# Attention in an MoE kernel: the last V product contracts over 128 rows, one group of maxima moves behind the first V product, high parts are made a head ahead, the division moves into odd heads

## The chip, the cores and the metric

The kernel runs on one core of a Trainium2 chip. The metric is the device time of one execution in microseconds (us); less is better. Five engines work side by side, each through its own program in order: TensorE (PE, matrix products; its weight loads are shown apart as PEld), VectorE (DVE), ScalarE (ACT), GpSimd (POOL) and SyncE (SP), which here issues the DMAs.

## The reference, cut to what matters

The program is a causal attention over blocks of 64 positions, an MoE with a cosine as its activation, and a second MoE with a normalised gate. The change touches the attention alone.

```python
def _attn_ref(q, k, v):                 # 4 batches, 8 heads, 576 positions, 64 wide
    scores = scale * np.matmul(q, k.transpose(0, 1, 3, 2))
    mask = block_i >= block_j           # blocks of 64
    scores = np.where(mask, scores, -1000000000.0)
    scores = scores - np.max(scores, axis=-1, keepdims=True)
    attn = np.exp(scores)
    attn = attn / (np.sum(attn, axis=-1, keepdims=True) + 1e-09)
    return np.matmul(attn, v)

x = attention laid out as (2304, 512)
h = x @ w_in; x = (h * np.cos(h)) @ w_out          # first MoE
out = sum over 8 experts of P[:, e] * (relu(x @ w1[e]) @ w2[e])   # second MoE
```

## The kernel before, in words

**Heads.** `attention()` walks the 32 heads (4 batches x 8) in one loop, `for i in range(NH)`, written out by hand: the order of the calls in its body is the order of the instructions on each engine, and semaphores do the rest. A head has 576 positions, that is four chunks of 128 keys and a fifth of 64. The scores stand transposed (keys in partitions, queries in columns), so a row sum comes out of the V product through a column of ones in `V`.

**Two passes for precision.** q and k are split into a high part in the short format that one PE pass takes (fp32r) and the rest. `high_parts(i)` makes the high parts of head `i` from the loaded tile `st[i]`: `HI` (both of them, ACT), `QA` (ACT), `KA` and `KB`'s lower half (two casts on POOL). `low_parts(i)` writes `QB = st - HI` on DVE. `move_q_hi` and `move_k_lo` bring halves to other partitions by DMA (`qb<-qa`, `kb<-qb`). The product of QB and KB (128 rows) and that of QA and KA (101 rows) add up in PSUM.

**The maxima** for head i+1 are found while head i is worked on. `peak(i + 1, 0)` and `peak(i + 1, 1)` are two groups of three short products into the one PSUM tile `px`; `find` reduces each with two and three instructions `nm<-px` on DVE. The second group writes over the first, so it waits for the first `find`. `turn` transposes the result on PE (`pt`), and `maxima` writes it, negated by a product with `diag`, into rows 96 to 100 of QA, where the QA-KA product subtracts it.

**Weights and V product.** `weights(i, 0..3)` compute the score tiles `sp`, `sq`, `sr` (512 columns each) and `sc` (the last 64 keys), and ACT takes their exponentials into `EP`, `EQ`, `ER` and `EC`. `pv(i, 0..4)` multiplies these by V. They are plain f32 products, so each counts twice in the trace (two passes). `EC` is a 64x64 tile, and its product uses 64 contraction rows. Even heads write 65 output rows, odd heads 128.

**Division.** `evac` copies a finished head from PSUM, `sums` sends its row sums to DRAM, `fetch`, `invert` and `give` take the reciprocals, `spread` brings them back over 64 partitions as `RB`, and `scale(e, h)` multiplies a head by them (DVE, two inputs in SBUF), for both heads of a pair. `x_hi` and `x_lo` split the outcome for the first MoE.

**Side work.** `conv_gen` converts the weights of the first MoE in small steps, of which `some(1)` issues the next: ACT `magnitude` together with the load of the next piece (`cw`, 512 KB, from SP), then ACT `rounding` and DVE `clamp`, then DVE `shift` and `bits`, then POOL `add`. One piece takes four steps, and four steps are issued per pair of heads. SP issues in each head, in program order: the `cw` load, V, two loads of q and k, `sums`, `qb<-qa`, `tt<-inv` (the spread), `kb<-qb`, as far as the head has them.

## Time and profile before

| | |
|---|---|
| Time, median of 3 runs | 2161.98 us (2161.3 to 2164.63) |
| The profiled execution's own time | 2162.53 us |
| Its span in the trace | 2160.7 us |
| PE busy | 2136.2 us (99%) |
| DVE, ACT, POOL busy | 1486.6, 961.9, 888.5 us (69%, 45%, 41%) |
| Chain that ended last | PE 86%, issue 5%, DVE 4%, POOL 3% |

The span runs from the first to the last instruction; the time of an execution holds 1.83 us more. Attention is the first tenth of the span: the first product of the MoE starts at 217.55 us. The granted PE clock is full in all slices of the page.

### The profile page before, as it was taken

The numbers are of one execution on the slowest core, as the hardware profiler recorded it, in microseconds if no ns is written. First come the engines' busy times: TensorE is split into PE (matmuls) and PEld (weight loads), VectorE is DVE, ScalarE is ACT, GpSimd is POOL, SyncE is SP. The second block draws the span as 40 slices with busy tenths as digits, with TensorE's granted clock in tenths as the row PEclk, the third lists the DMA queues.
The fourth block names the chain that finished last, engine by engine and source line by source line (L and its number), as shares of the span: only waits on it lengthen the run. The fifth ranks groups of instructions, "written<-read, shape, count | busy, mean of one in ns | idle before, by whom it ended". The sixth has DMA issues, their size and how long they took to land.

```text
span 2160.7 us, 29639 instructions
## 1 busy us (share of the span) xinstructions
PE 2136.2 (99%) x10869; PEld 1878.3 (87%) x10869; DVE 1486.6 (69%) x2445; ACT 961.9 (45%) x1795; POOL 888.5 (41%) x809
## 2 busy tenths in 40 slices
PE   8999999999999999999999999999999999999999
PEld 6666899998988889898888989888898888888898
DVE  7888677567667866666767666666766666666666
ACT  6777555434444433433444343444334344433432
POOL 3444444333324334344553434343563434344341
PEclk9999999999999999999999999999999999999999
DMA  6676220001002112121212212122122212212120
GB/s 157 181 182 170 65 69 20 7 1 40 1 22 70 66 60 78 59 79 59 73 65 88 78 59 79 59 72 66 60 77 88 78 59 71 67 61 77 59 78 30
DMA packets 74161, 152.84 MB, mean 71 GB/s; under 512 B 32896, under 2 KB 32896, under 8 KB 74016
## 3 DMA queue, kind: packets, MB, share of 16 engines
q1 hardware_dynamic: 74016, 150.95, 22.9%
q8 instruction: 86, 1.41, 0.3%
q14 instruction: 59, 0.48, 0.1%
HBM read 136.91 MB, written 4.87 MB: 66 GB/s over the span
## 4 chain that ended last, share of the span: by engine, by line
PE 86%; issue 5%; DVE 4%; POOL 3%; ACT 1%; DMA 1%; SPq 0%; POOLq 0%; ACTq 0%; DVEq 0%
PE acc L492 12%; PE acc L494 12%; PE acc L493 12%; PE hx L494 6%; PE hx L492 6%; PE hx L493 6%; PE acc L723 6%; PE hy L494 3%; PE hy L492 3%; PE hy L493 3%; POOL jl L68 2%; PE h L494 2%; PE h L492 2%; PE h L493 2%; PE hz L492 2%
## 5 line engine op out<-in xcount | busy, mean ns | idle before, releaser
L602 POOL TENSOR_TENSOR wv<-stg,wv 128x512 fp32r<-128x512 f32 x190 | 333.6, 1776 | 856.9 <-ACT wv L601 856.9
L492 PE MATMUL acc<-wv,hh 128*128 128x512 f32 x1152 | 456.5, 396 | 0.0
L494 PE MATMUL acc<-wv,hl 128*128 128x512 f32 x1152 | 455.5, 395 | 0.0
L493 PE MATMUL acc<-wv,hh 128*128 128x512 f32 x1152 | 454.5, 395 | 0.0
L897 DVE SCALAR_TENSOR_TENSOR oa<-acc,P,oa 128x512 f32<-128x512 f32 x540 | 379.0, 740 | 4.9 <-PE acc L494 4.3
L868 ACT ACTIVATE hh<-c 128x384 fp32r<-128x384 f32 x288 | 151.3, 525 | 409.5 <-DVE c L953 168.5
L869 DVE SCALAR_TENSOR_TENSOR hl<-c,hh 128x384 fp32r<-128x384 f32 x288 | 164.8, 572 | 176.1 <-ACT hh L868 176.1
L494 PEld LDWEIGHTS acc<-wv,hl 128*128 128x128 f32 x1152 | 216.0, 187 | 53.7
L493 PEld LDWEIGHTS acc<-wv,hh 128*128 128x128 f32 x1152 | 215.9, 187 | 43.9
L492 PEld LDWEIGHTS acc<-wv,hh 128*128 128x128 f32 x1152 | 216.1, 188 | 42.9
L68 POOL TENSOR_TENSOR jl<-raw,jh 128x512 fp32r<-128x512 f32 x95 | 132.2, 1393 | 190.0 <-ACT jh L65 178.2
L946 DVE TENSOR_TENSOR c<-hz,c 128x384 f32<-128x384 f32 x96 | 53.4, 557 | 193.9 <-PE hz L494 193.9
L593 DVE TENSOR_TENSOR wal<-s,wah 128x1024 fp32r<-128x1024 f32 x96 | 171.4, 1786 | 0.0
L936 ACT ACTIVATE c<-hx 128x384 f32<-128x384 f32 x95 | 46.9, 493 | 275.7 <-PE hx L494 275.7
L494 PE MATMUL hy<-xh,wal 128*128 128x384 f32 x384 | 128.8, 336 | 1.0 <-DVE wal L593 1.0
L492 PE MATMUL hy<-xh,wah 128*128 128x384 f32 x384 | 128.9, 336 | 0.6 <-DVE c L953 0.4
L492 PE MATMUL hx<-th,wah 128*128 128x384 f32 x384 | 128.6, 335 | 0.5 <-ACT c L936 0.5
L494 PE MATMUL hx<-th,wal 128*128 128x384 f32 x384 | 128.5, 335 | 0.0
L493 PE MATMUL hy<-xl,wah 128*128 128x384 f32 x384 | 128.3, 334 | 0.0
L493 PE MATMUL hx<-tl,wah 128*128 128x384 f32 x384 | 128.3, 334 | 0.0
L492 PE MATMUL h<-xh,jh 128*128 128x384 f32 x376 | 126.4, 336 | 0.5 <-PE h L494 0.5
L494 PE MATMUL h<-xh,jl 128*128 128x384 f32 x376 | 126.3, 336 | 0.4 <-POOL jl L68 0.4
(223 smaller groups left out, 4741.5 us busy)
## 6 DMA issues: line engine op xcount, KB each, us to landing
stg<-in_w_b_dram SPq DMA_DIRECT2D x192, 512.0 KB
cw<-in_w_a_dram SPq DMA_DIRECT2D x32, 512.0 KB
st<-in_qk_dram SPq DMA_DIRECT2D x64, 144.0 KB
v<-in_v_dram SPq DMA_DIRECT2D x31, 160.0 KB
tt<-inv SPq DMA_DIRECT2D x32, 144.0 KB
out_dram<-oa SPq DMA_DIRECT2D x18, 256.0 KB
kb<-qb SPq DMA_DIRECT2D x31, 144.0 KB
qb<-qa SPq DMA_DIRECT2D x31, 144.0 KB
```

The source lines that it names most:

```text
L68: eng_lo.tensor_tensor(out=lo, in0=src, in1=hi.bitcast(F32), op=ALU.subtract)
L492: nc.tensor.matmul(ps, lh, rh, start=first, stop=False, skip_group_check=go_on)
L493: nc.tensor.matmul(ps, lh, rl, start=False, stop=False, skip_group_check=go_on)
L494: nc.tensor.matmul(ps, ll, rh, start=False, stop=last, skip_group_check=go_on)
L593: eng.tensor_tensor(out=self.al, in0=self.s, in1=self.ah.bitcast(F32), op=ALU.subtract)
L602: eng.tensor_tensor(out=t[:, DM:2 * DM], in0=src, in1=t[:, 0:DM].bitcast(F32), op=ALU.subtract)
L723: nc.tensor.matmul(acc[half, b][:, at:at + w_], w[:, s], h[:, t0:t0 + w_], start=f == 0 and i == 0 and at == 0, stop=f == F1 - 1 and i == ...
L868: nc.scalar.activation(hh, src, AF.Relu)
L869: nc.vector.scalar_tensor_tensor(out=hl, in0=src, scalar=0.0, in1=hh.bitcast(F32), op0=ALU.max, op1=ALU.subtract)
L897: nc.vector.scalar_tensor_tensor(out=o, in0=acc, scalar=p, in1=o, op0=ALU.mult, op1=ALU.add)
L936: nc.scalar.activation(c[0], x, AF.Copy)
L946: nc.vector.tensor_tensor(out=c[0], in0=z, in1=c[0], op=ALU.add)
```

## The change

1. `EC` becomes one fixed tile of 128 rows, whose lower 64 rows are zeroed once by POOL; the last V product contracts over all 128 rows.
2. The second group of maxima (`peak(i + 1, 1)`) is issued behind `pv(i, 0)`, not ahead of it, and `pt` behind the product with the first part of `ER`, one product later than before.
3. `HI` is made by a function of its own, `high_both(i + 3)`, at the end of ACT's work in head i: the high part for a head is ready one head ahead. `low_parts(i + 2)`, which needs it, stands ahead of the second `find`.
4. Both `scale` calls stand in odd heads, one ahead of `low_parts`, one behind `maxima`.
5. The weight conversion has five steps a piece, the clamp being one of its own, and five are issued per pair of heads; they move so that the clamp falls in even heads, `add` and the `cw` load in odd heads. In the first MoE `some(4)` becomes `some(5)`.

```diff
@@ -136,8 +136,9 @@
                 if 0 < k < NHALF - 1:
                     self.load(k + 1)
                 yield
+                self.clamp(k)
+                yield
                 self.rounding(k)
-                self.clamp(k)
                 yield
                 self.shift(k)
                 self.bits(k)
@@ -166,6 +167,8 @@
             HI = p1.tile([128, S], F32R, name="hi")
             NM = [p1.tile([128, 101], F32, name=f"nm{j}") for j in range(2)]
             diag = p1.tile([128, 640], BF16, name="diag")
+            EC = p1.tile([128, D], F32, name="ec")
+            nc.gpsimd.memset(EC[64:128, :], 0.0)
 
             V = [p1.tile([128, 5, D + 1], F32, name="v0"), p1.tile([128, 5, 2 * D], F32, name="v1")]
             VC = [slice(0, D), slice(D, 2 * D)]
@@ -180,7 +183,7 @@
             conv = Conv(post.tile([128, 4 * DM], I32, tag="th", name="cw", bufs=1), tla[:, 0:DM].bitcast(I32))
             conv_gen = conv.run()
             SC = top.tile([72, 2, 8], F32, name="sc8")
-            st, EP, EQ, ER, EC, SUMS, INV, ps_t, ps_o = ({} for _ in range(9))
+            st, EP, EQ, ER, SUMS, INV, ps_t, ps_o = ({} for _ in range(8))
 
             def some(n):
                 for _ in range(n):
@@ -242,8 +245,10 @@
                 nc.gpsimd.memset(V[1][:, :, 0:D], 0.0)
                 nc.gpsimd.memset(V[1][:, :, 0:1], 1.0)
 
+            def high_both(i):
+                nc.scalar.activation(HI, st[i], AF.Copy)
+
             def high_parts(i):
-                nc.scalar.activation(HI, st[i], AF.Copy)
                 nc.scalar.activation(QA[i % 2][0:64, 64:640], st[i][64:128, :], AF.Copy)
                 nc.gpsimd.tensor_copy(out=KA[i % 2][0:64, :], in_=st[i][0:64, :])
                 nc.gpsimd.tensor_copy(out=KB[i % 2][64:128, :], in_=st[i][0:64, :])
@@ -332,8 +337,7 @@
                 else:
                     ps = pst.tile([128, 512], F32, tag="c", name="sc")
                     scores(ps[:, 0:256], i, 4, 320, 256)
-                    EC[i] = p1.tile([64, 64], F32, tag="ec", name="ec")
-                    nc.scalar.activation(EC[i], ps[0:64, 192:256], AF.Exp, scale=0.125)
+                    nc.scalar.activation(EC[0:64, :], ps[0:64, 192:256], AF.Exp, scale=0.125)
 
             def pv(i, c):
                 m = D + 1 if i % 2 == 0 else 2 * D
@@ -354,7 +358,7 @@
                     nc.tensor.matmul(o[:, 832:1024], vt[:, 3], ER.pop(i)[:, 320:512], start=False, stop=True,
                                      skip_group_check=True)
                 else:
-                    nc.tensor.matmul(o[:, 960:1024], vt[0:64, 4], EC.pop(i), start=False, stop=True,
+                    nc.tensor.matmul(o[:, 960:1024], vt[:, 4], EC, start=False, stop=True,
                                      skip_group_check=True)
 
             def evac(i):
@@ -416,6 +420,7 @@
             tiles()
             find(*px)
             find(*peak(0, 1))
+            high_both(1)
             high_parts(1)
             ones_of_v()
             turn(0)
@@ -433,8 +438,6 @@
                     load(i + 3)
                 if i:
                     sums(i - 1)
-                if even and i:
-                    some(1)
                 if nxt:
                     move_q_hi(i + 1)
                 if even and i >= 4:
@@ -443,37 +446,48 @@
                     find(*peak(i + 1, 0))
                 for part in range(4):
                     weights(i, part)
+                    if i == 0 and part == 0:
+                        high_both(2)
                 if odd and i >= 3:
                     invert(i - 3)
                     give(i - 3)
                 if odd and i >= 5:
-                    scale(i - 5, 1)
+                    scale(i - 5, 0)
+                if even and i:
+                    some(1)
+                if nxt2:
+                    low_parts(i + 2)
+                    move_k_lo(i + 2)
+                pv(i, 0)
                 if nxt:
                     find(*peak(i + 1, 1))
                 if nxt2:
                     high_parts(i + 2)
                 if even and i >= 2:
                     fetch(i - 2)
-                if nxt2:
-                    low_parts(i + 2)
-                    move_k_lo(i + 2)
+                if odd and i > 1:
+                    some(1)
                 if even and i >= 6:
                     x_hi(i - 6)
                     x_lo(i - 6)
+                if odd or i:
+                    some(1)
+                if i + 3 < NH:
+                    high_both(i + 3)
                 if i == NH - 1:
                     split(*spare, raw[0][:, 0:DM], nc.scalar, nc.gpsimd)
-                some(1)
-                pv(i, 0)
                 pv(i, 1)
+                pv(i, 2)
                 if nxt:
                     turn(i + 1)
                     maxima(i + 1)
-                for c in range(2, 5):
-                    pv(i, c)
-                if even and i >= 4:
-                    scale(i - 4, 0)
-                if odd:
+                pv(i, 3)
+                pv(i, 4)
+                if odd and i >= 5:
+                    scale(i - 5, 1)
+                if even and i:
                     some(1)
+            some(3)
             evac(NH - 1)
             sums(NH - 1)
             e = NH - 2
@@ -781,7 +795,7 @@
                         gb = times(pb, rb)
                         g_hi(n, 1, gb)
                         g_lo(n, 1, gb)
-                        some(4)
+                        some(5)
                     else:
                         wsplit(n - 1, 1)
                         open_group(0)
```

What it moves on PE, shown for head 21 (an odd head): from the end of its scores (`sc`) to the scores of the next head. `px` is the maxima tile, `o` the output of the V product. Before:

```order
L312 MATMUL sc<-qa_99,ka_101 64x256
L278 MATMUL px<-ka_100,qa_98 128x256
L278 MATMUL px<-ka_100,qa_98 128x320
L278 MATMUL px<-ka_100,qa_98 128x256
L345 MATMUL o<-ep,v_111 128x512
L346 MATMUL o<-eq,v_111 128x64
L348 MATMUL o<-eq,v_111 128x448
L299 MATMUL pt<-ident,nm_107 101x128
L351 MATMUL o<-er,v_111 128x320
L354 MATMUL o<-er,v_111 128x192
L357 MATMUL o<-ec,v_111 128x64
L278 MATMUL px<-ka_101,qa_99 128x256
```

After, in the same place:

```order
L317 MATMUL sc<-qa_99,ka_101 64x256
L349 MATMUL o<-ep,v_113 128x512
L350 MATMUL o<-eq,v_113 128x64
L283 MATMUL px<-ka_100,qa_98 128x256
L283 MATMUL px<-ka_100,qa_98 128x320
L283 MATMUL px<-ka_100,qa_98 128x256
L352 MATMUL o<-eq,v_113 128x448
L355 MATMUL o<-er,v_113 128x320
L304 MATMUL pt<-ident,nm_107 101x128
L358 MATMUL o<-er,v_113 128x192
L361 MATMUL o<-ec,v_113 128x64
L283 MATMUL px<-ka_101,qa_99 128x256
```

The three `px` products stand two V products later, and only two V products are left behind `pt`, where there were three.

On DVE, one pair of heads, from the first `find` of an odd head (two `nm<-px`) on; `tt` is the target of a scale, `qb<-st,hi` the low part, `qa<-pt,diag` the maxima. Before:

```order
L294 TENSOR_REDUCE nm_107<-px 128x1 x2
L375 RECIPROCAL sc_119<-sc_119 72x16
L392 TENSOR_TENSOR tt<-raw,tt 64x576
L294 TENSOR_REDUCE nm_107<-px 128x1 x3
L253 TENSOR_TENSOR qb_103<-st,hi 128x576
L113 TENSOR_SCALAR tla<-tla 128x512
L303 TENSOR_TENSOR qa_98<-pt,diag 5x640
L117 TENSOR_SCALAR tla<-tla 128x512
L124 SCALAR_TENSOR_TENSOR raw<-cw,tla 128x512
L294 TENSOR_REDUCE nm_108<-px 128x1 x5
L253 TENSOR_TENSOR qb_102<-st,hi 128x576
L303 TENSOR_TENSOR qa_99<-pt,diag 5x640
```

After:

```order
L299 TENSOR_REDUCE nm_107<-px 128x1 x2
L379 RECIPROCAL sc_121<-sc_121 72x16
L396 TENSOR_TENSOR tt<-tla,tt 64x576
L258 TENSOR_TENSOR qb_103<-st,hi 128x576
L299 TENSOR_REDUCE nm_107<-px 128x1 x3
L308 TENSOR_TENSOR qa_98<-pt,diag 5x640
L396 TENSOR_TENSOR tt<-raw,tt 64x576
L299 TENSOR_REDUCE nm_108<-px 128x1 x2
L113 TENSOR_SCALAR tla<-tla 128x512
L258 TENSOR_TENSOR qb_102<-st,hi 128x576
L299 TENSOR_REDUCE nm_108<-px 128x1 x3
L308 TENSOR_TENSOR qa_99<-pt,diag 5x640
```

The low part moves ahead of the second `find` (`x3`) in both heads; the odd head gets a scale ahead of it and gives clamp, shift and bits to the even head.

On POOL, the same pair: `raw<-raw,cw` is the conversion's `add`, `xl<-tt,xh` is `x_lo`. Before:

```order
L130 TENSOR_TENSOR raw<-raw,cw 128x512
L248 CAST ka_100<-st 64x576
L249 CAST kb_104<-st 64x576
L399 TENSOR_TENSOR xl<-tt,xh 128x576
L248 CAST ka_101<-st 64x576
L249 CAST kb_105<-st 64x576
```

After:

```order
L253 CAST ka_100<-st 64x576
L254 CAST kb_104<-st 64x576
L403 TENSOR_TENSOR xl<-tt,xh 128x576
L253 CAST ka_101<-st 64x576
L254 CAST kb_105<-st 64x576
L130 TENSOR_TENSOR raw<-raw,cw 128x512
```

The `add` moves from ahead of the casts of the even head to right behind those of the odd head (`ka_101`, `kb_105`).

## Rows read from the trace of the kernel before

**Rows 1.** One line of the code: durations, first and last start, heads 5 to 30.

```profile
L278 PE MATMUL px<-ka,qa x153: 278/362/400, 45.0 to 206.5; 68*128 68x256 f32 x76, 68*128 68x448 f32 x26, 68*128 68x512 f32 x26, 68*128 68x320 f32 x25
```

**Rows 2.** Timeline, PE, heads 19 and 20: start us, us, line, operation, [idle before].

```profile
135.22 0.82 PE L278 MATMUL px<-ka,qa 68*128 68x256 f32 x3
135.89 0.40 PE L311 MATMUL sp<-qb,kb 128*128 128x512 f32 x1
136.12 0.40 PE L312 MATMUL sp<-qa,ka 101*128 101x512 f32 x1
...
137.67 0.28 PE L312 MATMUL sc<-qa,ka 101*64 101x256 f32 x1
137.89 0.62 PE L278 MATMUL px<-ka,qa 68*128 68x256 f32 x3
138.35 1.02 PE L345 MATMUL o<-ep,v 128*128 128x512 f32 x2
139.21 0.33 PE L346 MATMUL o<-eq,v 128*128 128x64 f32 x2
139.38 0.97 PE L348 MATMUL o<-eq,v 128*128 128x448 f32 x2
...
140.83 0.49 PE L354 MATMUL o<-er,v 128*128 128x192 f32 x2
141.25 0.43 PE L357 MATMUL o<-ec,v 64*128 64x64 f32 x2
141.61 0.81 PE L278 MATMUL px<-ka,qa 68*128 68x256 f32 x3
...
144.05 0.28 PE L312 MATMUL sc<-qa,ka 101*64 101x256 f32 x1
144.39 0.62 PE L278 MATMUL px<-ka,qa 68*128 68x256 f32 x3
...
146.57 0.27 PE L299 MATMUL pt<-ident,nm 128*101 128x128 f32 x1
...
147.90 0.38 PE L278 MATMUL px<-ka,qa 68*128 68x256 f32 x1
```

**Rows 3.** Timeline, DVE, heads 19 to 21.

```profile
136.46 1.29 DVE L294 TENSOR_REDUCE nm<-px 128x1 f32<-128x448 f32 x2
...
137.93 0.76 DVE L392 TENSOR_TENSOR tt<-raw,tt 64x576 f32<-64x576 f32 x1
138.70 0.89 DVE L294 TENSOR_REDUCE nm<-px 128x1 f32<-128x192 f32 x3
...
140.91 0.83 DVE L303 TENSOR_TENSOR qa<-pt,diag 5x640 fp32r<-5x640 f32 x1
...
142.95 1.29 DVE L294 TENSOR_REDUCE nm<-px 128x1 f32<-128x448 f32 x2
...
146.88 0.83 DVE L303 TENSOR_TENSOR qa<-pt,diag 5x640 fp32r<-5x640 f32 x1 [0.29 <-PE pt L299]
...
150.70 1.27 DVE L392 TENSOR_TENSOR tt<-tt 64x576 f32<-64x576 f32 x1
```

**Rows 4.** Timeline, POOL, heads 19 to 21.

```profile
138.02 1.19 POOL L248 CAST ka<-st 64x576 fp32r<-64x576 f32 x1 [2.45 <-PE sc L312]
...
143.15 1.31 POOL L130 TENSOR_TENSOR raw<-raw,cw 128x512 int32<-128x512 int32 x1 [3.23 <-DMA kb<-qb]
...
150.69 0.66 POOL L248 CAST ka<-st 64x576 fp32r<-64x576 f32 x1 [2.27 <-PE sc L312]
```

**Rows 5.** Chain of waits between 30 and 46 us (heads 3 and 4).

```profile
32.18 0.76 PE px L278 x3
...
34.98 4.56 DMA qb<-qa
```

**Rows 6.** Timeline, ACT, head 0.

```profile
17.51 0.68 ACT L246 ACTIVATE hi<-st 128x576 fp32r<-128x576 f32 x1 [1.26 <-DMA st<-in_qk_dram]
```

**Rows 7.** Timeline, PE, head 0.

```profile
17.70 0.28 PE L346 MATMUL o<-eq,v 128*65 128x64 f32 x2
```

## The prediction

> **What bounds the kernel now.** Attention is the only stage that the change touches in substance. (In the first MoE a call issues five steps in place of four, and a piece has five in place of four: the same work in the same calls, which I cost at nothing.) I read the views in this order. First the line of the `px` products, which start every head: from head 5 they start at 45.0, and the last three of them, head 30's, end their starts at 206.5 [rows 1]. Three starts lie some 0.43 us apart in all (135.22 to 135.89 less the 0.23 of the last, [rows 2]), so 25 heads take 161.1 us, 6.44 each, **12.89 us a pair** of an odd and an even head. Heads 5 to 29 are 12.5 such pairs. Second PE's timeline of one pair, heads 19 and 20 [rows 2]: PE runs nearly without a break, so what counts is not idle time but products that start later than their size explains. Two places show that. At `sc` to `px` the step is 0.22 us in head 19 (137.67 to 137.89) and 0.34 in head 20 (144.05 to 144.39), where 256 columns need 0.12 (half the 0.23 that 512 take, 135.89 to 136.12): the second `px` group waits until DVE has read the first. And around `ec`, the only product with 64 contraction rows: the two 192-column passes ahead of it take 0.42 us (140.83 to 141.25), it takes 0.36 itself (141.25 to 141.61) though two passes of 64 columns with 128 rows take 0.17 (139.21 to 139.38), and the three `px` behind it take 0.67 (135.22 to 135.89) for 1216 columns that need 0.56 at the rate of 512 in 0.23. Third DVE and POOL of the same heads [rows 3, 4], since after the change they decide whether PE can keep what it saves.
>
> **Part 1, 128 rows for ec.** Two passes of 512 such columns take 0.86 us (138.35 to 139.21), so two of 192 need 0.32 to 0.33: that run shrinks from 0.42 to 0.33, ec from 0.36 to 0.17, and px by 0.11: **0.39 us a head**. POOL zeroes the lower half of the tile once, ahead of the heads. The page "TensorEngine Tiling (Array Packing)" of the Trainium skill, Key Properties, has it that a change of tiling mode drains TensorE, which is what these three rows look like. Against the change speaks "TensorE: Matmul & The Clock Gate" of the Trainium skill, whose table under "Why this matters for your kernels" gives a single product of few rows the time of one with 128; by that the edit would save nothing (rival C), and the rows so far bear out the first page.
>
> **Part 2, the px group behind the first V product.** The wait goes: find of the first group ends at 137.75 (136.46 + 1.29, [rows 3]), 2.5 us into the head, and the group now starts some 3.5 us into it. Saved 0.10 in head 19 and 0.22 in head 20. With both parts and no new wait head 19 takes 6.39 - 0.39 - 0.10 = 5.90, head 20 6.29 - 0.39 - 0.22 = 5.68 [rows 2], **a pair 11.58**. What is late next is the second find, since `pt` waits for it, and behind pt only 0.61 us of PE work are left (0.11 of its own, 0.33 and 0.17), where 1.33 were (146.57 to 147.90).
>
> **Parts 3 and 4, DVE in the even head.** The order is find, clamp, low, find, maxima, shift, bits. The low part waits for `sc` and for HI, which was made a head ago. KA starts 0.35 us behind the last `sc` product (137.67 to 138.02, [rows 2, 4]), 2.70 into the head, and takes 0.66 alone (150.69). Clamp stands in no row, but KA's end, not clamp, sets when low can go; low ends some 0.62 behind KA (the price of that just below), near 4.0, the second find of 0.89 near 4.9, pt could start at 5.05 and PE gets there at 5.07 (5.68 - 0.61): **no wait, 5.68 us**.
>
> **DVE in the odd head** is the long one. The chain begins with the even head's pt: 0.31 to maxima (146.57 to 146.88, [rows 2, 3]), 2.04 for maxima, shift and bits (140.91 to 142.95), 1.47 for find and reciprocal (136.46 to 137.93): the first scale is ready 3.82 us behind pt, or 3.2 to 3.3 us into the odd head. There it meets POOL: KA 2.70 to 3.36, KB from 3.41 to 4.07. In the rows the two don't share time: the scale of 0.76 us takes 1.27 where KA began 0.01 ahead of it (150.70 against 150.69) and ends 0.62 behind KA's end; KA takes 1.19 in place of 0.66 where the scale began first (138.02 against 137.93) and ends 0.52 behind the scale's end [rows 3, 4]. So scale ends at 3.98, KB at 4.50, low (the same kind of operation with two inputs) at 5.12, the second find at 6.04, pt follows 0.14 later (as px followed find, 137.75 to 137.89) at 6.18, and the head takes **6.79 us**. The second scale and POOL's add (1.31 us, 143.15) come behind and hold nobody: add starts at 5.1, and the scale only at 7.3. A pair is then 5.68 + 6.79 = **12.47**. The page "SBUF — State Buffer" of the Trainium skill, Who interferes with whom, says that such a pair excludes each other for the whole instruction; that would be 0.76 in place of 0.62 and 0.66 in place of 0.52, a pair near 12.9 and no gain, and the rows show the shorter times.
>
> **Part 5, the late qb.** The load of cw now stands ahead of the even head's loads, so the qb of the next odd head queues behind it. Where the queue was full, qb was issued 2.80 us into the head and took 4.56 to land, 7.36 behind the head's start, and the chain runs through it [rows 5]: the next head's sp waited. Head 19 shows no such wait, with 7.06 us of room (6.39 and the 0.67 of px), so its qb landed earlier. After, the odd head's sp wants it at 5.68 + 0.56 = 6.24. Its stall s is between 0 and 1.1 us, and I have no row nearer. It doesn't simply add up, as DVE has slack against it in part: for s = 0.5, KA runs 3.20 to 3.86, scale ends at 4.48, KB at 5.00, low at 5.62, find at 6.54, pt at 6.68, the head takes 7.29 and **the pair 12.97**. For s = 1, scale is ahead of KA, low takes its turn between KA and KB and ends near 5.15, and PE itself is the limit with 5.90 + 1.0: a pair near 12.6. I take the middle of the ends, **12.72, or 0.17 below before**.
>
> **Head 0** pays for `high_both(2)`: ACT has it behind the first exponential, and its input lands so late that it runs from 17.51 to 18.19 [rows 6]; the second exponential ends at most one such duration later, 18.87, and the eq product starts at 18.96 in place of 17.70 [rows 7], with the px group of 0.46 us (137.89 to 138.35 is its length elsewhere) still to come: 1.26 + 0.46 - 0.39 = **+1.3 us**.
>
> **Heads 1 to 4** have no scale and no spread, and PE is the limit. Heads 3 and 4 took 12.82 (32.18 to 45.0, [rows 1, 5]) and would take 11.58 and a stall s, so 0.1 to 1.2 less; I take 0.7, and the same for heads 1 and 2: **-1.4**. The last two heads I cost at nothing; what they save and their extra steps of the conversion bound that at twice part 1's 0.39 either way.
>
> **Sum.** +1.3 - 1.4 - 12.5 x 0.17 = -2.2 us. The profiled execution took 2162.53, 1.83 more than its span and 0.55 more than the median of the runs shown; 2160.3 for it is 2159.8 as a median.
>
> **Rival A, the odd head isn't held.** If POOL's casts and DVE's operations hit each other less than in these two rows (casts later by a stall, or a chain that is a little quicker), low ends at 3.25 + 2 x 0.77, near 4.8, pt starts at 5.85 and the head takes 6.46: a pair 12.14, -9.4 over 12.5 pairs, 2152.5 in all. With PE as the only limit, 11.58, it is -16.4 and 2145.5. For it: DVE's work is nearly equal in both heads now. Against it: scale and KA come within half a microsecond by the sum of measured durations.
>
> **Rival B, slower: add gets between scale and low.** If the first scale is ready only when KB has begun, at 3.41, that is from 0.15 us later than I reckon, POOL's add queues behind KB at 4.1 while scale still holds the ports. KB ends at 4.07, scale at 4.69, add goes first and ends near 5.86 (1.31 less the 0.14 that a held cast gained), low at 6.48, find at 7.40, pt at 7.54, the head takes 8.15: a pair 13.83, +0.94, +11.8 in all pairs, near 2173.5; in half of the pairs near 2167. For it: the margin is small, and a late `sums` would delay the reciprocal ahead of the scale. Against it: every delay of sp by qb moves POOL the other way.
>
> **Rival C, ec saves nothing.** Then both heads keep 0.39 more: a pair 13.4 to 13.5, +0.56, with next to nothing won in heads 1 to 4: about 2170. Against it stand the three starts in rows 2 that no other product shows.
>
> **How the numbers follow.** What I forecast (held, with s somewhere in its range) gets 0.46; its own range is 2156.6 (pair 12.47) to 2163 (12.97). A gets 0.26 with 2145.5 to 2154, B 0.20 with 2167 to 2174, C 0.08. A measurement of this kernel can tell about 0.2%, 4.3 us: faster is below 2157.7, slower above 2166.3. Faster is A and a fifth of the forecast's chance, 0.36; slower is B and C, a point lower for a half-way B, 0.27; the rest is 0.37. The range leaves out the far end of A and the top of B: 2150 to 2173.
>
> **What the profile after would show.** ec's two passes at 0.17 us and px behind it at 0.56 (part 1). No step above 0.12 us from sc to the next product, and no wait of px for nm (part 2). Odd heads near 6.8 to 7.3 with PE waiting at pt for the second find, even heads near 5.7 without a wait. The first scale and low of odd heads at 0.9 to 1.3 us; about 1.7 for low would be rival B, 0.76 for both rival A. A wait of the odd heads' sp for qb of up to 1.1 us. Head 0 longer by 1.3. Wrong would be the whole if even heads were the long ones, or if ACT, whose order the change alters too, came to hold the products.

## The result: slower by half a per cent

The changed kernel takes 2173.43 us (median of four runs, 2170.25 to 2175.38), the kernel before 2162.53 in the same comparison: a ratio of 1.0051, 95% interval 1.0037 to 1.0065. The forecast was 2159.8. The profiled execution took 2174.71 us, 12.2 more than that of before. Where the 12.2 lie follows from both traces. A head is counted from the last of the three `px` starts that open it, and the MoE from its first product:

| us | before | after | change | forecast |
|---|---|---|---|---|
| head 0 | 8.42 | 11.24 | +2.8 | +1.3 |
| heads 1 to 4 | 25.14 | 23.44 | -1.7 | -1.4 |
| heads 5 to 29 | 161.08 | 169.73 | +8.7 | -2.1 |
| heads 30, 31 | 11.0 | 10.65 | -0.35 | 0 |
| from the MoE's first product on | 1943.2 | 1945.9 | +2.7 | 0 |

So the rows for heads 1 to 4 and for heads 5 to 29 part: the gain of the first came, and the largest loss lies where a gain of 2 us was expected. The line of the `px` products in heads 5 to 29 and head 30's start shows the stretch that [rows 1] shows of before; it is longer.

```profile
L283 PE MATMUL px<-ka,qa x153: 280/363/561, 46.3 to 216.4; 68*128 68x256 f32 x76, 68*128 68x448 f32 x26, 68*128 68x512 f32 x26, 68*128 68x320 f32 x25
```

PE's timeline of an even head and the start of the odd head behind it (start us, us, line, operation, what the idle time ahead of it waited for), to be held against [rows 2]:

```profile
136.31 0.28 PE L317 MATMUL sc<-qa,ka 101*64 101x256 f32 x1
136.43 1.02 PE L349 MATMUL o<-ep,v 128*65 128x512 f32 x2
...
139.14 0.28 PE L304 MATMUL pt<-ident,nm 128*101 128x128 f32 x1
139.26 0.49 PE L358 MATMUL o<-er,v 128*65 128x192 f32 x2
139.58 0.28 PE L361 MATMUL o<-ec,v 128*65 128x64 f32 x2
139.67 0.80 PE L283 MATMUL px<-ka,qa 68*128 68x256 f32 x3
141.58 0.47 PE L316 MATMUL sp<-qb,kb 128*128 128x512 f32 x1 [1.10 <-DMA qb<-qa]
```

Parts 1 and 2 do most of what they should. From `sc` to the next product it is 0.12 us (136.31 to 136.43) and not 0.22 to 0.34; the 192-column passes take 0.32 (139.26 to 139.58) and not 0.42; ec takes 0.09 (139.58 to 139.67), and 0.14 in odd heads. Then the odd head's `sp` starts 1.91 us behind its `px`, where 0.64 is the usual step in this trace. Two lines of PE's waits between 46.2 and 216.5 us sum this up (us in total, times, longest):

```profile
PE sp L316 <- DMA qb<-qa: 12.1, 10, 1.6
PE pt L304 <- DVE nm L299: 2.0, 5, 0.6
```

Even heads take 5.92 us on average, most of them 5.78. Odd heads take 7.59. Eleven of the thirteen odd heads from 5 to 29 wait for a transfer (ten for `qb<-qa`, one for `tt<-inv`). Counted as what the step from px to sp takes beyond 0.64, they lose 0.66 to 1.80 us there, 15.0 in all. The chain of waits goes through that transfer, as it did in one head of before [rows 5]:

```profile
137.55 3.89 DMA qb<-qa
141.44 0.14 issue
141.58 0.47 PE sp L316
```

Ahead of the transfer stands a wait of the queue that issues it. The cw load overwrites the half of `cw` that the conversion's `add` reads, one step before it, and the change puts both behind the odd head's casts. SP issues in order, so V, q, k and `qb` stand behind the load while it waits. POOL and SP around the start of head 18 (133.89), and SP's waits on that line, after (46 to 217 us) and before (46 to 207):

```profile
133.20 1.29 POOL L130 TENSOR_TENSOR raw<-raw,cw 128x512 int32<-128x512 int32 x1
134.52 0.37 SPq L90 DMA_DIRECT2D cw<-in_w_a_dram  x1
137.55 0.48 SPq L264 DMA_DIRECT2D qb<-qa  x1
SPq L90 <- POOL raw L130: 24.0, 13, 2.1
SPq L90 <- POOL xl L399: 0.4, 1, 0.4
```

In the nine even heads in which the load is issued only after their start (4, 6, 8, 10, 16, 18, 20, 24, 28), the next odd head waits 1.26 to 1.80 us for a transfer. Behind the four others (12, 14, 22, 26), where it is issued earlier, it waits 0, 0, 0.66 and 1.07.

In three of the eleven heads (11, 21 and 25, of 8.98 to 9.34 us) something comes on top of the wait. The table by stretches of head 11 (core us; PE, PEld, DVE, ACT and POOL busy with their counts; the granted PE clock; the DMA share; GB/s):

```profile
87.30:89.20 1.90, 0.34 (x2) 0.00 (x0) 1.80 (x4) 0.66 (x2) 0.00 (x0) 1.00 0.89 199
89.20:91.00 1.80, 1.77 (x10) 1.64 (x11) 1.38 (x4) 1.53 (x4) 0.00 (x0) 0.98 0.74 193
91.00:94.00 3.00, 3.00 (x10) 1.94 (x8) 1.00 (x2) 2.92 (x6) 2.14 (x3) 0.50 0.57 134
94.00:96.00 2.00, 2.00 (x9) 1.37 (x9) 0.97 (x4) 0.00 (x0) 0.90 (x1) 0.91 0.11 26
```

PE stands still for most of 1.9 us, works on at the full clock for 1.7, and then has half of it granted (0.50, the level of 1.2 GHz) for 3.4 us. Heads 21 and 25 show the same, and head 7, which waited as long, doesn't (same columns; head 7 behind its wait, then the stretches in heads 11, 21 and 25):

```profile
61.70:67.00 5.30, 5.27 (x28) 4.02 (x28) 3.30 (x9) 4.47 (x9) 2.89 (x3) 1.00 0.64 146
90.95:94.30 3.35, 3.35 (x12) 2.28 (x11) 1.05 (x2) 2.98 (x6) 2.44 (x3) 0.50 0.57 134
155.80:159.20 3.40, 3.40 (x11) 2.39 (x10) 1.61 (x3) 2.68 (x6) 1.21 (x2) 0.50 0.65 134
183.15:186.50 3.35, 3.35 (x12) 2.81 (x12) 1.93 (x4) 2.10 (x6) 0.37 (x1) 0.50 0.84 154
```

Such a head is 1.6 to 1.7 us longer than its wait explains, about half of 3.4; the three make 4.9 us.

### The profile page after: what moved, and what is told of

Same layout as the page of the kernel before. It is cut to its first block, busy times and chain, and to the rows that moved or that the text cites. A ratio compares the mean times of both kernels' runs of the same rounds, so it can differ in the third digit from the quotient of the medians.

```text
span 2172.9 us, 29623 instructions
## 1 busy us (share of the span) xinstructions
PE 2133.0 (98%) x10869; PEld 1880.4 (87%) x10869; DVE 1491.6 (69%) x2445; ACT 961.9 (44%) x1795; POOL 902.8 (42%) x810
## 4 chain that ended last, share of the span: by engine, by line
PE 84%; issue 5%; DVE 3%; DMA 3%; POOL 3%; ACT 2%; SPq 0%; ACTq 0%; POOLq 0%; DVEq 0%
PE acc L506 12%; PE acc L508 12%; PE acc L507 12%; PE hx L508 6%; PE hx L506 6%; PE hx L507 6%; PE acc L737 6%; PE hy L508 3%; PE hy L506 3%; PE hy L507 3%; POOL jl L68 2%; DMA qb<-qa 2%; PE h L508 2%; PE h L506 2%; PE h L507 2%
```

## The experiments

Two theories stood against each other. **Q**: the transfers. The cw load stands in front of the shorter even heads' loads, so the odd heads' qb lands late. **L**: DVE and POOL. The odd head's scale and low are held by the casts (or by `add`), and pt waits for the second find. The table gives each run's median, its ratio to the kernel before in its own comparison with the interval, and from its trace the heads in us: the means of odd and even heads, heads 5 to 29 over 12.5 as the pair, and head 0. In these comparisons the kernel before had medians of 2161.5 to 2162.5, so a difference between two medians of the table holds to about 1 us.

| run | us | ratio, interval | odd, even head | pair | head 0 |
|---|---|---|---|---|---|
| before | 2162.53 | | 6.50, 6.38 | 12.89 | 8.42 |
| after | 2173.43 | 1.0051, 1.0037 to 1.0065 | 7.59, 5.92 | 13.58 | 11.24 |
| ec_alone | 2157.88 | 0.9981, 0.9972 to 0.9991 | 6.25, 6.42 | 12.66 | 8.09 |
| ec_px | 2167.71 | 1.0027, 1.0014 to 1.0039 | 6.00, 7.04 | 13.00 | 7.43 |
| ec_undone | 2174.65 | 1.0062, 1.0041 to 1.0082 | 7.64, 6.06 | 13.76 | 9.81 |
| load_late | 2186.58 | 1.0109, 1.0093 to 1.0126 | 7.97, 6.73 | 14.75 | 11.07 |
| load_end | 2169.24 | 1.0037, 1.0022 to 1.0051 | 6.84, 6.48 | 13.34 | 9.58 |
| load_end_h0 | 2170.50 | 1.0034, 1.0018 to 1.0049 | 6.67, 6.89 | 13.54 | 9.05 |
| qb_first | 2172.60 | 1.0047, 1.0031 to 1.0062 | 7.53, 5.95 | 13.54 | 9.53 |
| load_small | 2159.26 | 0.9990, 0.9980 to 0.9999 | 6.81, 5.78 | 12.63 | 9.63 |
| small_scales | 2157.50 | 0.9979, 0.9969 to 0.9988 | 5.87, 6.57 | 12.41 | 11.43 |
| scales_only | 2165.46 | 1.0018, 1.0009 to 1.0028 | 6.56, 6.57 | 13.12 | 9.65 |
| split | 2162.85 | 1.0006, 0.9997 to 1.0016 | 6.83, 5.82 | 12.69 | 9.54 |
| split_scales | 2158.65 | 0.9989, 0.9979 to 0.9998 | 5.94, 6.62 | 12.54 | 9.03 |
| split_scales_q | 2159.02 | 0.9988, 0.9979 to 0.9998 | 6.01, 6.58 | 12.56 | 8.93 |
| clamp_hole | 2160.76 | 0.9995, 0.9986 to 1.0004 | 6.72, 6.03 | 12.78 | 8.95 |
| ec_split | 2163.19 | 1.0004, 0.9995 to 1.0013 | 6.71, 6.33 | 13.06 | 7.42 |

**The transfer taken away.** load_small is the changed kernel with an eighth of each cw load behind the first two; the rest of those weights it leaves out:

```diff
-            nc.sync.dma_start(out=self.w64[i], in_=src[:, (k % 2) * DM:(k % 2 + 1) * DM, :])
+            n = DM if i < 2 else DM // 8
+            nc.sync.dma_start(out=self.w64[i][:, 0:n, :], in_=src[:, (k % 2) * DM:(k % 2) * DM + n, :])
```

> The changed kernel with an eighth of each cw load (64 KB in place of 512 KB; the weights of the first MoE are wrong), nothing moved. Theory Q: no wait for qb in the odd heads; what is left is the odd head's own chain on DVE and POOL: 2150 to 2160 us. Theory L: the odd heads stay at 7.2 or more, 2168 to 2174 us. The load of the first MoE's stage shrinks too, which has waits for it nowhere in the profile.

2159.26 us: 13 to 14 below the changed kernel, with no wait for qb left. SP's wait for `add` falls with it, from 24.0 to 7.7 us, so this run doesn't part the bytes ahead of qb from the time at which they are issued. What remains is what theory L describes, at the size that the prediction worked out. DVE in an odd head of this run that begins at 131.71 (start us, us, line, operation):

```profile
133.54 1.29 DVE L300 TENSOR_REDUCE nm<-px 128x1 f32<-128x448 f32 x2
134.75 0.24 DVE L380 RECIPROCAL sc<-sc 72x16 f32<-72x16 f32 x1
134.91 0.81 DVE L397 TENSOR_TENSOR tt<-tla,tt 64x576 f32<-64x576 f32 x1
135.65 1.21 DVE L259 TENSOR_TENSOR qb<-st,hi 128x576 fp32r<-128x576 f32 x1
136.78 0.87 DVE L300 TENSOR_REDUCE nm<-px 128x1 f32<-128x192 f32 x3
```

POOL beside it, and pt on PE in the same run:

```profile
134.45 0.66 POOL L254 CAST ka<-st 64x576 fp32r<-64x576 f32 x1 [2.25 <-PE sc L318]
135.17 1.08 POOL L255 CAST kb<-st 64x576 fp32r<-64x576 f32 x1
```

```profile
137.80 0.33 PE L305 MATMUL pt<-ident,nm 128*101 128x128 f32 x1 [0.65 <-DVE nm L300]
```

KA ends at 135.11 and scale at 135.72, 0.61 later; KB ends at 136.25, 0.53 behind scale; low ends at 136.86, 0.61 behind KB; pt follows at 137.80, 6.09 into the head (6.18 was reckoned), and the head takes 6.72 (6.79). Ten of the twelve pairs take about 12.5, where the forecast's case without a stall said 12.47. One is shorter (an odd head of 6.28); in the other exception, an odd head of 8.06 us, scale started 0.06 behind the start of KB, `add` got in ahead of low, and low took 1.83 us:

```profile
160.26 1.21 DVE L397 TENSOR_TENSOR tt<-tla,tt 64x576 f32<-64x576 f32 x1 [0.20 <-POOL ka L254]
161.40 1.83 DVE L259 TENSOR_TENSOR qb<-st,hi 128x576 fp32r<-128x576 f32 x1
```

That is rival B of the prediction, in one head.

**The scales moved.** In small_scales and scales_only the first scale goes behind maxima, to the second; in the first with the small load, in the second with the load as the change has it:

```diff
-                if odd and i >= 5:
-                    scale(i - 5, 0)
                 if even and i:
                     some(1)
...
                 if odd and i >= 5:
+                    scale(i - 5, 0)
                     scale(i - 5, 1)
```

> The changed kernel with an eighth of each cw load, as in the run before, and the first scale of the odd head moved behind maxima, next to the second. With the small load alone odd heads took 6.73 to 6.76 with 0.82 us of wait at pt for the second find, even heads 5.78. If that wait is the first scale and low held by POOL's casts, it goes: odd heads 5.9, a pair 11.7, even heads at most 0.3 longer, as the scales now run into them; 2147 to 2151 us. If it is something else in the chain (the maxima of the even head, the find), odd heads stay above 6.4: 2156 to 2160.

> The changed kernel with nothing but the first scale moved behind maxima; the cw load whole and where the change put it. Theory Q: in the odd heads the wait for qb and the wait of pt for the second find cover each other, so with the late qb left as it is, the shorter DVE chain brings little: odd heads still wait 1 to 2 us for qb, 2166 to 2173 us. If the DVE chain was the larger cost all along: 2158 to 2163, as with both mended (2158.7).

With the small load, odd heads come to 5.87 us: the wait of pt was indeed the scale and low held by the casts. But even heads go to 6.57 (at most 0.3 more was expected), with 0.64 of wait at pt, since the scales now run into them and push low onto KB. The pair gains 0.1 beside the 12.51, and 2157.50 is not the 2147 to 2151 of the expectation. DVE's work is moved from one head of the pair to the other: a pair takes 12.4 to 12.5 us either way, and PE waits for the second find in one of its two heads. With the whole load, the same move gives 2165.46, 7 to 8 us below the changed kernel and slightly better than expected: the longer even heads give qb more time to land, so that odd heads wait 0.26 to 0.87 us in most cases (2.15 in one) and not 0.66 to 1.80. So that run doesn't separate the theories; in it the two waits cover each other in part.

**The cw load moved.** load_late issues it one step later, load_end two, and load_end_h0 has besides the high part of head 2 back behind the four exponentials of head 0:

```diff
                 self.magnitude(k)
-                if 0 < k < NHALF - 1:
-                    self.load(k + 1)
                 yield
+                if 0 < k < NHALF - 1:      # load_late
+                    self.load(k + 1)
                 self.clamp(k)
                 yield
+                if 0 < k < NHALF - 1:      # load_end
+                    self.load(k + 1)
                 self.rounding(k)
```

> The changed kernel with the cw load issued one step later, in the even head behind qb and tt, instead of at the end of the odd head. Theory Q: the waits of the odd heads' sp for qb (11 us on PE in heads 5 to 30) go or shrink to under 3 us, and with them the three stretches at the half clock; odd heads 6.4 to 6.8, 2158 to 2163 us. Theory L: the waits may go, but the odd heads stay at 7.2 or more because pt then waits for the second find; 2170 to 2174 us.

> The changed kernel with the cw load two steps later: at the end of the even head, behind qb, tt, kb and the fetch of the sums, where the kernel before has it. Moving it one step, ahead of the fetch, took the odd heads' wait for qb away but made the reciprocal wait for the sums (13.7 us on DVE), and 2186.6 us came of it. Theory Q, now: the transfers are served in turn, and what stands behind cw is late; behind the fetch it is the even head's qb, which has the whole odd head to land. No wait for sums, few for qb; odd heads 6.4 to 6.8, 2156 to 2163 us. Theory L: pt of the odd heads waits for the second find by 0.8 us or more without any wait for a transfer, 2163 to 2172 us.

> As the kernel with the load at the even head's end, and the high part of head 2 in head 0 again behind all four exponentials, as before. Head 0 took 11.24 us in the changed kernel against 8.42 before, so 2 to 3 us less than its twin, by either theory.

load_late came out at 2186.58, slower than anything else, and against both theories' numbers. The odd heads' wait for qb is gone, but the fetch of the sums now stands behind the load, and the odd head's DVE begins with what needs it (DVE, same columns):

```profile
152.83 0.25 DVE L379 RECIPROCAL sc<-sc 72x16 f32<-72x16 f32 x1 [2.79 <-DMA sc<-sums]
153.00 0.69 DVE L396 TENSOR_TENSOR tt<-tla,tt 64x576 f32<-64x576 f32 x1
153.61 0.74 DVE L258 TENSOR_TENSOR qb<-st,hi 128x576 fp32r<-128x576 f32 x1
```

Scale and low take 0.69 and 0.74 here, as POOL is long done; they are merely late, and pt waits up to 3.1 us (21.4 in all, 12 times). Much of the time above the changed kernel is the clock's: 0.92 is granted on average from 46 to 231 us, where the changed kernel has 0.97 from 46.7 to 216.4. load_end, behind the fetch, has 2169.24: odd heads mostly 6.73 to 6.76 as reckoned without a stall, even heads now waiting for qb (up to 1.9 us, in a head of 10.54 with the half clock behind it), and ACT waiting 17.8 us in all for cw itself. So in each of the three places that were tried something waits for the load or behind it; that part of theory Q holds, while its hope that the odd head gives qb time enough failed. load_end_h0 doesn't differ from its twin (the intervals overlap nearly wholly); head 0 is 0.5 us shorter in its trace and not 2 to 3.

**qb moved, load cut.** qb_first issues `move_q_hi(i + 1)` as the first transfer of a head, ahead of V and of the loads of q and k. split issues half of the cw load (256 KB) at the odd head's end and half behind the fetch of the even head; split_scales joins it with the moved scales and head 2's old place of the high part; split_scales_q issues qb behind V besides; clamp_hole is split_scales with the even head's clamp behind the second find:

```diff
+                if nxt:
+                    move_q_hi(i + 1)       # qb_first; split_scales_q: behind load_v
                 if i:
                     evac(i - 1)
...
-                    self.load(k + 1)
+                    self.load(k + 1, (0,))         # split
...
+                if 0 < k < NHALF - 1:
+                    self.load(k + 1, (1,))
                 self.rounding(k)
...
-                if even and i:
-                    some(1)
                 if nxt2:
                     low_parts(i + 2)
...
                     find(*peak(i + 1, 1))
+                if even and i:
+                    some(1)                        # clamp_hole
```

> The changed kernel with the qb transfer issued first in every head, ahead of V and of the loads of q and k, the cw load where the change put it. Theory Q: qb lands earlier by the 448 KB that stood in front of it, but has still the cw load ahead of it and waits for the kb transfer of the head before; the odd heads' wait shrinks by half or more, 2160 to 2168 us. Theory L: 2170 to 2174 us. A third outcome is a wait of ACT's high part for q and k, which land later: up to 2175 us.

> The changed kernel with the cw load cut in two: 256 KB at the odd head's end, where the change has all 512, and 256 KB at the even head's end, behind the fetch. Theory Q: the odd heads' qb has 256 KB less in front of it, so their waits of 1.25 to 1.8 us shrink to under 0.6; with the odd heads' own chain at 6.75 a wait of that size costs up to 0.5 a pair; 2158 to 2165 us. If the waits come from the number of transfers and not their bytes, nothing is won: 2172 or more.

> As the cut load, with the first scale behind maxima and the high part of head 2 back behind the exponentials. If both causes are what they seem, PE becomes the limit: odd heads 5.9 plus the wait for qb, which a shorter pair makes longer again; 2150 to 2160 us. If qb takes back all that DVE gives, 2158 to 2165.

> As the kernel before it in this list, with the qb transfer issued behind V and ahead of the two loads of q and k. It has 288 KB less in front of it, so no head waits for it; instead the high part, which wants the q and k loaded in the same head, may wait on ACT and hold the copy of the finished head behind it. 2146 to 2156 us without that, 2160 to 2172 with it.

> The cut cw load, the scale behind maxima and head 2's high part behind the exponentials (2158.7), and in even heads the clamp moved from ahead of low to behind the second find, where DVE waits 0.51 us for pt anyhow. Even heads took 6.57 with 0.64 of wait at pt. If DVE's own order is what is left, they come to 6.1 to 6.3 and the time to 2152 to 2157 us; if qb takes it back as the pair shortens, or low still meets KB, 2157 to 2161.

qb_first, 2172.60, wins nothing, and its third outcome came: the wait moves to ACT, where the high part of the next head waits for q and k loaded behind qb, with the exponentials behind it (44.9 us of wait, 22 times, up to 3.5), and late sums hold the reciprocal too. split has 2162.85, 10 to 11 below the changed kernel, no transfer wait over 0.9 us and odd heads of 6.3 to 7.1 but for one of 8.07. The number of transfers went up and the wait down, so it isn't their number that makes qb late; the bytes ahead of it are halved, and SP's wait for `add` is too (12.5 us). With the scales it is 2158.65, with qb earlier 2159.02, alike. clamp_hole shortens the even heads from 6.62 to 6.03 and lengthens the odd ones by 0.78: `sp` now waits for `maxima` (5.8 us, 11 times), which clamp delays. It gains nothing (2160.76).

**The parts alone.** ec_alone is the kernel before with part 1, ec_px with parts 1 and 2, ec_undone the changed kernel without part 1. ec_split is ec_alone with the load cut in two. The edit of part 1 is the change's own; that of ec_px:

```diff
+                pv(i, 0)
                 if nxt:
                     find(*peak(i + 1, 1))
...
-                pv(i, 0)
                 pv(i, 1)
+                pv(i, 2)
                 if nxt:
                     turn(i + 1)
                     maxima(i + 1)
-                for c in range(2, 5):
+                for c in range(3, 5):
                     pv(i, c)
```

> The kernel before with part 1 alone: ec as a fixed tile of 128 rows, everything else in the old order. Both theories have the same PE saving, 0.39 us a head where PE is the limit, so at most 12.5 us over 32 heads; the odd head's DVE work (about 6.5 us) takes part of it back through the wait of the second px group. Theory Q (the loss of the changed kernel is the late qb transfer, because the cw load stands in front of the shorter even heads): heads of 5.9 to 6.5 us, 2153 to 2158 us. Theory L (the loss is DVE and POOL holding each other in the odd heads): the same, since the old order of DVE and POOL stays. If 128 rows saved nothing: 2162.

> The kernel before with parts 1 and 2: ec at 128 rows, the second px group behind the first V product, pt one product later; DVE, ACT, POOL and SP in the old order. ec alone gave 2157.9. Either theory: the wait of px for the first find goes (0.3 us a head on average), but low and clamp follow the second find on DVE and pt has less room, so a part comes back; a faster head also makes qb of even heads late, as ec alone showed four times (0.4 to 0.9 us). 2152 to 2158 us; over 2160 if the late second find costs more than the px wait did.

> The changed kernel with ec at 64 rows again. Theory Q: even heads longer by 0.39 us (6.17), which gives qb that much more room, so the odd heads' wait is shorter by as much; the odd heads get 0.39 behind the wait: a pair longer by 0.4, 2176 to 2180 us, unless the shorter stalls end the stretches at the half clock, then 2171 to 2174. Theory L: 2178 to 2183 us, 0.78 a pair. If 128 rows saved nothing: 2173.

> The kernel before with part 1 alone, and the cw load cut in two halves, one at the end of the even head and one at the end of the odd head. ec alone took 2157.9, with four waits of the even heads' sp for qb of 0.4 to 0.9 us and waits of px for the first find of 0.3 to 0.8. If the transfers stand in the way as in the changed kernel, the waits for qb go and 2 to 3 us with them, 2154 to 2157 us; if the other half now makes the odd heads' qb late, 2157 to 2160.

ec_alone, 2157.88, is faster than before by 0.09 to 0.28%: 128 rows save PE time, but of the 0.39 us a head that were reckoned only 0.12 are kept. A part was never there (the `px` term, see the next section); the rest goes back to DVE (px waits 0.3 to 0.8 us for the first find or the reciprocal in sixteen places) and to qb (four waits of the even heads). ec_px takes px's wait away and is 10 us slower than ec_alone: with odd heads of 5.95 to 6 us but for one, every even head from 6 to 28 waits for qb (PE's waits between 46 and 207 us):

```profile
PE sp L313 <- DMA qb<-qa: 10.7, 12, 2.0
```

So a loss of this kind needs neither the new place of the cw load nor the new order on DVE; a head shorter than the way of the transfer that its successor wants is enough. Here too that way begins with the issue: SP issues qb 3.50 us into an odd head on average, and 2.47 in the kernel before. ec_undone can't be told from the changed kernel (the intervals overlap). A reading that fits, and that nothing else here tests: while qb sets the odd head's start, what PE saves ahead of that wait comes back as wait. ec_split, meant to free ec_alone's qb, is no faster than before; four waits for qb stay, and `tt<-inv` now lands late, so that DVE waits for it (12.0 us, 10 times).

No run is clearly faster than ec_alone (small_scales leaves work out, and the intervals of the two split_scales runs overlap with it). It beats both kernels, by 0.19% the one before. Wherever the load stands apart from `add` (load_late and load_end; SP's waits on that line make 0.8 and 0.3 us in all), the odd heads don't wait for qb; but no run frees it from `add` in the change's own place, so how much of the loss hangs on that wait alone is open.

## Why the prediction was wrong

- **What bounds attention, parts 1 and 2**: right but for one term. 0.12 at `sc`, 0.32 and 0.09 around ec; even heads 5.78 where 5.68 was reckoned, and odd heads 5.87 where nothing holds them (small_scales; 5.90 was reckoned). The 0.11 that px was to gain behind ec didn't come: px to sp takes 0.64 with 128 rows (133.89 to 134.53) where it took 0.67. In even heads ec had taken 0.26 in the kernel before (147.64 to 147.90) and not 0.36, so part 1 is worth about 0.3 us a head. The first line is of before, the others of after:

```profile
147.64 0.33 PE L357 MATMUL o<-ec,v 64*65 64x64 f32 x2
133.75 0.33 PE L361 MATMUL o<-ec,v 128*128 128x64 f32 x2
133.89 0.81 PE L283 MATMUL px<-ka,qa 68*128 68x256 f32 x3
134.53 0.39 PE L316 MATMUL sp<-qb,kb 128*128 128x512 f32 x1
```

- **Even head without a wait**: right within 0.1 us in most heads; in three of twelve pt waited 0.54 for the find.
- **Odd head's chain**: right, to 0.1 us at each of its steps (load_small), but mostly covered in the changed kernel: there pt waits in two odd heads and three even ones, 2.0 us of PE idle time in all.
- **Part 5, the late qb**: here the forecast failed. The stall s was put between 0 and 1.1 us, by one row of before and the absence of others, and the middle of the *pair's* ends was taken, 12.72, because DVE's slack made a stall of 1 look cheaper than one of 0.5. Measured, ten odd heads waited for qb and one for tt by 0.66 to 1.80 us, 1.36 on average over those eleven. The time to land was right: about 4.5 us on average in the ten (3.89 in the chain above), where the one row had 4.56. What was off is the issue: 3.3 us into the even head on average, and not 2.80. The prediction says of `add` that it holds nobody; in the trace it holds the cw load, and with it every later issue of SP, for 24.0 us in 13 waits. By the prediction's own formula for a stall above 1, 5.68 + 5.90 + s, that alone gives a pair of 12.9, no gain at all. The DMA share over heads 5 to 29 is 0.71 before and 0.72 after, so on average there was room; what counted was when, within a pair, the bytes were issued.
- **A term that was missing**: the half clock behind three of the waits, 4.9 us, where the kernel before has 1.00 granted from 20 us to the end of attention. Two more stretches at 0.50 stand in head 0 and in the MoE (below). The clock isn't the whole loss: the four executions of the changed kernel had 0.996, 0.997, 0.999 and 0.997 on average, and that at 0.999 still took 2170.25 us.
- **Head 0**: right, but for the clock. ACT's high part ran from 17.52 to 18.20 as reckoned, the eq product started at 18.74 (18.96 reckoned, 17.70 before, [rows 7]), and then the clock fell (0.57 granted between 18.7 and 22.5): head 0 is 2.8 longer and not 1.3. In load_small, load_end, scales_only and split, which have the same head 0, the clock stays at 1.00 there and the head takes 9.54 to 9.65, 1.1 to 1.2 more than before.

```profile
18.74 0.33 PE L350 MATMUL o<-eq,v 128*65 128x64 f32 x2 [1.87 <-ACT eq L330]
```

- **The MoE at nothing**: wrong by 2.7 us. One wait of 1.6 us is new (PE's waits from 227 us on), and the granted clock is 0.98 in the first 102 us of the stage, where it was 1.00; all of that is one stretch (0.52 granted from 241.0 to 244.5):

```profile
PE h L506 <- DVE g L713: 1.6, 1, 1.6
```

  The wait stays with the small load (1.2 us), so the bytes of the load aren't its cause; five steps a call instead of four may be, but no run tried that alone. In load_end and scales_only, with the full clock there, the stage takes 1944.4 us, 1.2 more than before. So some 1.5 of the 2.7 go with the clock, and the cause of the rest is open.
- **Rival B named the time, 2173.5, but not the cause.** `add` between scale and low was seen in one head of load_small. A right number that another mechanism made is no support for it.
- The Trainium skill's page "TensorEngine Tiling (Array Packing)", Key Properties, is borne out against the other page weighed there, in two of the three late starts: with 128 rows they are gone ahead of ec and at it (0.42 to 0.32, and 0.36 to 0.14 in odd heads, 133.75 to 133.89). The third, px behind ec, went from 0.67 to 0.64 only, so ec's rows were not what held it; what did is open.

The sum over heads 5 to 29, from PE alone (13 x 5.88 + 12 x 5.78 = 145.8 us) to 169.7: transfers 15.0, half clock 4.9, pt behind the find 2.8; 1.2 are not placed. The step of the prediction that failed is thus the stall s of part 5. It was bounded at 1.1 us from one issue of qb at 2.80 us, with `add` holding nobody; eleven of thirteen odd heads lost 1.36 on average and up to 1.80.

## What to carry to other kernels

Before an engine's saving is counted, walk through one turn of the issuing queue in order: what does each issue wait for, when does that come in the shorter turn, and what stands ahead of each transfer that is waited for? The average wouldn't have shown it here (a DMA share of 0.71 and 0.72). A wait for qb that held one head of the kernel before by 0.6 us [rows 5] held ten of the changed one, and moving the load only picked what is late. Where a wait's size is known from one row only, work out both of its parts, issue and landing, for the new order, and don't take the middle of the outcomes. Take the part that pays by itself: here one line of the change gave all that there was to win.

## What the runs showed of the hardware

Behind a wait of PE the clock may fall, and the length of the wait alone doesn't tell whether it does: in heads 11, 21 and 25 PE waited 1.74, 1.52 and 1.46 us, worked on at full clock for 1.7, 1.0 and 0.5 us, and then had the lower level (0.50, 1.2 GHz) granted for 3.4 us; head 7 waited 1.80 us and the clock stayed at 1.00. A DVE operation with two SBUF inputs that meets a POOL cast ended 0.61 us behind the cast's end, and a cast that waited for it 0.53 behind its end, in each of the cases shown; that price, read from two rows of before (0.62 and 0.52), held to 0.01 us in another order of instructions.
